# The last two stores of a kernel, written as four: one transfer for each batch

## The chip, the cores and the metric

The kernel runs on one core of a Trainium2 chip, as one program. The metric is the device time of that program in microseconds (us), taken as the median of several executions. One execution was also recorded by the hardware profiler; every duration below is from that record, and times inside it count from the start of its span.

## The reference

The inputs are float32. A linear attention without a softmax over 4 batches, 8 heads, 576 tokens and a head size of 64 is normalised per head, its heads are laid side by side to 2304 rows (4 batches of 576 tokens) of 512 columns, and two feed-forward layers follow:

```
kv  = einsum('bhsd,bhse->bhde', k, v)
o   = einsum('bhsd,bhde->bhse', q, kv)
o   = o / sqrt(mean(o*o, -1) + 1e-6) * g_norm
x   = o.transpose(0, 2, 1, 3).reshape(2304, 512)
g   = x @ w_gate;  h = g * sigmoid(g) * (x @ w_val);  x = h @ w_out        # inner width 1536
h   = x @ w_in;    y = softplus(h) @ w_out2                                # inner width 2048
```

The output is `y`, 2304 rows of 512 float32 numbers (2 KB a row); row `b*576 + s` is token `s` of batch `b`.

## The kernel before, in words

A batch has 576 tokens, which is 4 x 128 and 64 over. The kernel works on five token groups: groups 0 to 3 are the first 512 tokens of each batch (`T` = 512), and group 4 (`t == B`, with `B` = 4) is made of the four remainders, 64 tokens of each batch (`REM` = 64), 256 tokens side by side. In group 4, tokens 0 to 63 belong to batch 0, 64 to 127 to batch 1, and so on.

The stages are: attention, woven with the first feed-forward layer; the rest of that layer; and the second layer. The second layer runs over pairs of slices of its inner width (`jp`), for two batches at a time, and adds each slice's product into an accumulator in on-chip memory, `zacc`. For one step `m` of `ffn2_o`, TensorE makes a tile `pz` of 128 tokens by 512 columns in six matrix multiplications (L788 to L792, issued in the helper at L436), and VectorE adds it to `zacc` (L796). After the last pair (`jp == F2 // 2 - 1`) each step also puts a store into the queue of deferred work (L809, L810), which is released by the planner's clock just behind the addition.

The store has two forms. For a whole batch, L806 and L807 write the 128 rows of a step (for batches 2 and 3) or the 512 rows of four steps (for batches 0 and 1) in one transfer. For the remainders, `m` is 0 or 1 and the 128 partitions of `av[:, m, :]` hold 64 tokens of batch `2m` and 64 of batch `2m + 1`. L800 views the output as batches by tokens by columns, and L801 writes both remainders in one transfer. Group 4 comes last of all, so the two transfers of L801 are the last instructions of the kernel but the end of the program (L1002).

All stores and weight loads are issued on SP, in program order. SP waits before an issue where the program says so (for the data, and for a completion counter that an earlier transfer used: there are eight of these, `DMAHW0` to `DMAHW7`, used in turn).

Of the kernel before, what the change touches and what calls it, by code (L numbers as in the profile page):

```python
# [71 lines left out]
def tile_linear_attention_two_ffn(  # L72
# [19 lines left out]
    nc = tc.nc  # L92
    P = 128
    B, H, S, D = q.shape
    NP = H // 2
    NC = S // P
    REM = S - NC * P
# [4 lines left out]
    T = NC * P  # L102
# [26 lines left out]
    def defer(dt, f):  # L129
        heapq.heappush(queue, (now[0] + dt, next(serial), f))  # L130
# [8 lines left out]
    def need(made, key):  # L139
        while key not in made:  # L140
            heapq.heappop(queue)[2]()
        return made[key]
# [288 lines left out]
    def mm3(dst, steps, first=True, last=True, lo_rhs_last=True, check=True):  # L431
        n = 3 * len(steps)
        i = 0
        for (ah, al), (bh, bl) in steps:
            for a, b_ in ((ah, bh), (al, bh), (ah, bl)) if lo_rhs_last else ((ah, bh), (ah, bl), (al, bh)):
                nc.tensor.matmul(  # L436
                    dst, lhsT=a, rhs=b_, start=first and i == 0, stop=last and i == n - 1,
                    skip_group_check=not check)
                i += 1
        tick(n * 0.216 * dst.shape[-1] / 512)  # L440
# [17 lines left out]
    def acc_tile(gen, t):  # L458
        if (gen, t) not in acc:
            acc[gen, t] = accp.tile([P, KD, widths[t]], F32, tag=f"acc{t}", name=f"{gen}acc{t}")  # L460
        return acc[gen, t]
# [316 lines left out]
    def ffn2_o(jp, t):  # L778
        w = widths[t]
        gs = {}  # L780

        def step(m):
            if m == 0:
                for k_ in range(2):
                    gs[k_] = us2.pop((2 * jp + k_, t)), need(wt, ("p", 2 * jp + k_))
            a = acc_tile("z", t)
            av = a.rearrange("p k w -> p (k w)").rearrange("p (m e) -> p m e", e=DM)
            p = po.tile([P, DM], F32, tag="po", name=f"pz{jp}_{t}_{m}")  # L788
            mm3(p, [
                (tuple(g[:, m * P:(m + 1) * P] for g in gs[k_][0]), gs[k_][1])  # L790
                for k_ in range(2)
            ], lo_rhs_last=False)  # L792
            if jp == 0:
                nc.vector.tensor_copy(av[:, m, :], p)
            else:
                defer(ADD2, lambda: nc.vector.tensor_add(av[:, m, :], av[:, m, :], p))  # L796

            def store():
                if t == B:
                    rows = out.rearrange("(b s) e -> b s e", b=B)  # L800
                    nc.sync.dma_start(rows[2 * m:2 * m + 2, T:S, :], av[:, m, :])  # L801
                else:

                    n = NC if t < 2 else 1
                    if (m + 1) % n == 0:
                        rows = out[t * S:t * S + T, :].rearrange("(p c) e -> p c e", p=P)  # L806
                        nc.sync.dma_start(rows[:, m + 1 - n:m + 1, :], av[:, m + 1 - n:m + 1, :])  # L807

            if jp == F2 // 2 - 1:  # L809
                defer(ADD2, store)  # L810

        return [lambda m=m: step(m) for m in range(w // P)]
# [17 lines left out]
    with tc.manual_schedule():  # L830
# [65 lines left out]
        for t in range(NT - 1):  # L896
            if t + 1 < B:
                b = t + 2
# [108 lines left out]
```

## Time and profile before

| | |
|---|---|
| time, median of 3 runs | 920.41 us (920.1 to 923.91) |
| the profiled execution's own time | 920.24 us |
| its span, from the first to the last instruction | 918.5 us |
| TensorE busy | 885.1 us, 96% of the span |
| VectorE busy | 588.8 us, 64% |
| ScalarE, GpSimd busy | 353.1 us, 288.4 us |
| transfers | 114.00 MB, mean 124 GB/s |

A busy share is an average over the span. A change that touches only the end of the program is to be read from the end of the timeline, from what the transfer engines do there, and from what the program's last instruction waits for. The profiled execution's time is 1.74 us longer than its span; that part lies outside of the record.

### The profile page before, as it was taken

How to read it: one execution, taken by the hardware profiler on the slowest of the kernel's cores; microseconds unless marked ns; L12 is line 12 of the kernel's file. 1: busy time of each engine (PE TensorE's matmuls, PEld its weight loads, DVE VectorE, ACT ScalarE, POOL GpSimd, SP SyncE). 2: the span in 40 equal slices, each digit the busy share in tenths (PEclk: the TensorE clock that was granted, in tenths of full speed). 3: DMA queues.
4: the chain of work that ended last, by engine and by line, in shares of the span. 5: the costliest groups of instructions: out<-in, count | busy, mean ns of one | idle time of the engine just before them, and what ended most of it. 6: DMA issues, size and time to landing. Idle time of an engine off the chain costs nothing.

```text
span 918.5 us, 11708 instructions
## 1 busy us (share of the span) xinstructions
PE 885.1 (96%) x4352; PEld 740.8 (81%) x4352; DVE 588.8 (64%) x916; ACT 353.1 (38%) x615; POOL 288.4 (31%) x216
## 2 busy tenths in 40 slices
PE   6889999999999999999999999999999999999994
PEld 5668888888888888888888878888877888888883
DVE  2955357867868686787776745566687555545552
ACT  3634435333332323233232543444455444343430
POOL 0633211313131313122131633344444443333440
PEclk9999999999999999999999999999999999999998
DMA  9975202143251605051534134444445433343102
GB/s 274 253 137 117 92 1 70 59 149 128 80 193 37 226 28 183 34 196 46 161 115 161 68 119 140 170 146 160 161 139 175 168 138 120 111 137 122 40 12 103
DMA packets 83932, 114.00 MB, mean 124 GB/s; under 512 B 27556, under 2 KB 56228, under 8 KB 83620
## 3 DMA queue, kind: packets, MB, share of 16 engines
q1 hardware_dynamic: 83716, 113.27, 38.6%
q8 instruction: 34, 0.56, 0.3%
q14 instruction: 22, 0.18, 0.1%
q10 hardware_dynamic: 160, 0.00, 0.0%
HBM read 91.75 MB, written 21.50 MB: 123 GB/s over the span
## 4 chain that ended last, share of the span: by engine, by line
PE 83%; DVE 6%; issue 3%; SPq 2%; POOL 2%; ACT 1%; DMA 1%; POOLq 0%; DVEq 0%; ACTq 0%
PE pz L436 20%; PE pv L436 15%; PE pg L436 15%; PE py L436 15%; PE hY L436 8%; PE hZ L436 4%; PE hr L436 2%; PE hX L436 2%; PE pa L366 1%; POOL b L620 1%; DMA qr<-in_q_dram 1%; PE kvp L318 1%; SPq L181 1%; DVE yacc L496 1%; POOL gl L698 1%
## 5 line engine op out<-in xcount | busy, mean ns | idle before, releaser
L496 DVE TENSOR_TENSOR yacc<-yacc,py 128x512 f32<-128x512 f32 (+1 forms) x220 | 136.4, 629 | 53.6 <-PE py L436 53.0
L796 DVE TENSOR_TENSOR zacc<-zacc,pz 128x512 f32<-128x512 f32 x126 | 85.9, 683 | 109.4 <-PE pz L436 109.2
L698 POOL TENSOR_TENSOR gl<-c,gh 128x512 fp32r<-128x512 f32 x64 | 88.5, 1383 | 189.7 <-ACT gh L697 145.4
L436 PE MATMUL pz<-pl,gh 128*128 128x512 f32 x288 | 112.5, 391 | 2.0 <-POOL pl L285 2.0
L436 PE MATMUL pz<-ph,gl 128*128 128x512 f32 x288 | 112.4, 390 | 0.6 <-POOL gl L698 0.6
L436 PE MATMUL pz<-ph,gh 128*128 128x512 f32 x288 | 112.4, 390 | 0.0
L478 ACT CAST uh<-u 128x512 fp32r<-128x512 f32 (+1 forms) x60 | 34.7, 578 | 173.8 <-DVE u L475 173.8
L436 PE MATMUL hY<-b,wh 128*128 128x512 f32 x384 | 97.6, 390 | 0.9 <-DVE c L726 0.9
L436 PE MATMUL py<-uh,oh 128*128 128x512 f32 (+1 forms) x240 | 89.7, 374 | 1.3 <-DVE yacc L496 1.3
L436 PE MATMUL pv<-xh,vh 128*128 128x512 f32 (+1 forms) x240 | 90.1, 375 | 0.0
L436 PE MATMUL pg<-xh,gh 128*128 128x512 f32 (+1 forms) x240 | 90.0, 375 | 0.0
L436 PE MATMUL pg<-xl,gh 128*128 128x512 f32 (+1 forms) x240 | 88.5, 369 | 0.5 <-DVE xl L404 0.5
L436 PE MATMUL py<-uh,ol 128*128 128x512 f32 (+1 forms) x240 | 88.6, 369 | 0.0
L436 PE MATMUL pv<-xh,vl 128*128 128x512 f32 (+1 forms) x240 | 88.6, 369 | 0.0
L436 PE MATMUL pg<-xh,gl 128*128 128x512 f32 (+1 forms) x240 | 88.5, 369 | 0.0
L436 PE MATMUL pv<-xl,vh 128*128 128x512 f32 (+1 forms) x240 | 88.4, 368 | 0.0
L436 PE MATMUL py<-ul,oh 128*128 128x512 f32 (+1 forms) x240 | 88.3, 368 | 0.0
L436 PEld LDWEIGHTS hY<-b,wh 128*128 128x128 f32 x384 | 71.6, 188 | 15.9 <-DVE c L726 1.3
L436 PEld LDWEIGHTS pz<-pl,gh 128*128 128x128 f32 x288 | 54.2, 188 | 13.2 <-POOL pl L285 2.9
L436 PEld LDWEIGHTS pz<-ph,gl 128*128 128x128 f32 x288 | 54.1, 188 | 13.0 <-POOL gl L698 1.8
L479 DVE TENSOR_TENSOR ul<-u,uh 128x512 fp32r<-128x512 f32 (+1 forms) x60 | 38.8, 647 | 39.1 <-ACT uh L478 39.1
L436 PEld LDWEIGHTS pz<-ph,gh 128*128 128x128 f32 x288 | 54.1, 188 | 10.9 <-ACT ph L282 0.3
(115 smaller groups left out, 1643.1 us busy)
## 6 DMA issues: line engine op xcount, KB each, us to landing
pr<-in_moe_w_out_dram SPq DMA_DIRECT2D x32, 512.0 KB, 4.3
wh<-w2d SPq DMA_DIRECT2D x32, 512.0 KB, 4.3
wh<-w2d SPq DMA_DIRECT2D x64, 256.0 KB, 2.9
ir<-in_moe_w_in_dram SPq DMA_DIRECT2D x16, 512.0 KB, 5.7
w2d<-kh SPq DMA_DIRECT2D x32, 256.0 KB, 2.0
w2d<-kl SPq DMA_DIRECT2D x32, 256.0 KB, 2.4
gr<-in_moe_w_gate_dram SPq DMA_DIRECT2D x12, 512.0 KB, 7.2
vr<-in_moe_w_val_dram SPq DMA_DIRECT2D x12, 512.0 KB, 7.2
```

The source lines that it names most:

```text
L181: nc.sync.dma_start(kr.rearrange("p h c d -> p h (c d)"), ks.rearrange("h (p c) d -> p h (c d)", p=P))
L318: nc.tensor.matmul(pk[:, hp, :], lhsT=kt[:, c, i:i + 2, :].rearrange("p h d -> p (h d)"), rhs=vt[:, i:i + 2, c * D:(c + 1) * D], start=(c ...
L366: nc.tensor.matmul(pv[p0:p0 + n, hp, :], lhsT=qt[:, hp, p0:p0 + n], rhs=kvm[bb][:, hp, :], start=True, stop=True,)
L436: nc.tensor.matmul(dst, lhsT=a, rhs=b_, start=first and i == 0, stop=last and i == n - 1, skip_group_check=not check)
L478: nc.scalar.copy(uh, u)
L479: (nc.gpsimd if UL1 == "g" else nc.vector).tensor_sub(ul, u, f32(uh))
L496: defer(ADD1, lambda: nc.vector.tensor_add(a[:, d, :], a[:, d, :], p))
L620: (nc.gpsimd if BLO[n][int(i[1])] == "g" else nc.vector).tensor_sub(t[:, 1], src(), f32(t[:, 0]))
L698: nc.gpsimd.tensor_sub(lo, l, f32(hi))
L796: defer(ADD2, lambda: nc.vector.tensor_add(av[:, m, :], av[:, m, :], p))
```

## The change

In the branch for the remainders, the one transfer of 128 rows is replaced by two transfers of 64 rows, one for each of the two batches in the tile. Each takes 64 partitions of `av[:, m, :]` and writes 64 neighbouring rows of the output, 128 KB. The branch runs twice (`m` = 0 and 1), so two transfers of 256 KB become four of 128 KB. The bytes and where they go are the same.

```
             def store():
                 if t == B:
-                    rows = out.rearrange("(b s) e -> b s e", b=B)
-                    nc.sync.dma_start(rows[2 * m:2 * m + 2, T:S, :], av[:, m, :])
+                    for i in range(2):
+                        r0 = (2 * m + i) * S + T
+                        nc.sync.dma_start(out[r0:r0 + REM, :], av[REM * i:REM * (i + 1), m, :])
                 else:
```

The end of SP's program before; `zacc_6515` and `zacc_6605` are the accumulators of batches 3 and 2, `zacc_5214` that of the remainders, the last figures are the shape of the transfer, and the brackets name the counters that SP waits for:

```order
L807 DMA out_dram<-zacc_6515 128x512 [waits DMAHW2_49,DVE_49]
L807 DMA out_dram<-zacc_6515 128x512 [waits DMAHW3_49,DVE_49]
L807 DMA out_dram<-zacc_6515 128x512 [waits DMAHW4_49,DVE_49]
L807 DMA out_dram<-zacc_6515 128x512 [waits DMAHW5_49,DVE_49]
L807 DMA out_dram<-zacc_6605 128x512 [waits DVE_49] x2
L807 DMA out_dram<-zacc_6605 128x512 [waits DMAHW0_49,DVE_49]
L807 DMA out_dram<-zacc_6605 128x512 [waits DMAHW1_49,DVE_49]
L801 DMA out_dram<-zacc_5214 2x64x512 [waits DMAHW2_49,DVE_49]
L801 DMA out_dram<-zacc_5214 2x64x512 [waits DMAHW3_49,DVE_49]
L1002 UNCONDITIONAL_BRANCH
```

And the same end of SP's program with the change (the lines of the source are one further on):

```order
L808 DMA out_dram<-zacc_6605 128x512 [waits DMAHW0_49,DVE_49]
L808 DMA out_dram<-zacc_6605 128x512 [waits DMAHW1_49,DVE_49]
L802 DMA out_dram<-zacc_5214 64x512 [waits DMAHW2_49,DVE_49]
L802 DMA out_dram<-zacc_5214 64x512 [waits DMAHW3_49]
L802 DMA out_dram<-zacc_5214 64x512 [waits DMAHW4_49,DVE_49]
L802 DMA out_dram<-zacc_5214 64x512 [waits DMAHW5_49]
L1003 UNCONDITIONAL_BRANCH
```

The last two entries became four. The first of each pair waits for VectorE's addition, the second only for a completion counter whose last user is eight transfers back. Nothing else moved on any engine.

## Rows read from the trace of the kernel before

**Rows 1.** The page's busy time by engine; the core's span and granted TensorE clock.

```profile
PE 885.1 (96%) x4352; PEld 740.8 (81%) x4352; DVE 588.8 (64%) x916; ACT 353.1 (38%) x615; POOL 288.4 (31%) x216
...
core 0: 918.5 us, clock 0.995
```

**Rows 2.** Timeline of the end: start us, us, engine, line, operation, tiles, [idle before].

```profile
904.46 0.39 PE L436 MATMUL pz<-ph,gl 128*128 128x512 f32 x1
904.88 0.69 DVE L796 TENSOR_TENSOR zacc<-zacc,pz 128x512 f32<-128x512 f32 x1 [0.67 <-PE pz L436]
...
902.88 0.33 SPq L807 DMA_DIRECT2D out_dram<-zacc  x1
...
904.24 0.66 SPq L801 DMA_DIRECT2D out_dram<-zacc  x1
...
905.60 0.53 SPq L801 DMA_DIRECT2D out_dram<-zacc  x1
```

**Rows 3.** What SP waited for at the end: us in total, times, longest.

```profile
SPq L1002 <- DMA out_dram<-zacc: 11.2, 1, 11.2
```

**Rows 4.** Stretches of the end: length, busy by engine, PEclk, DMA share, GB/s.

```profile
903.50:904.45 0.95, 0.95 (x5) 0.77 (x5) 0.69 (x1) 0.00 (x0) 0.00 (x0) 1.00 0.73 276
904.45:905.25 0.80, 0.40 (x2) 0.00 (x0) 0.36 (x1) 0.00 (x0) 0.00 (x0) 1.00 0.00 0
905.25:907.50 2.25, 0.00 (x0) 0.00 (x0) 0.32 (x1) 0.00 (x0) 0.00 (x0) 1.00 0.12 25
...
908.00:916.75 8.75, 0.00 (x0) 0.00 (x0) 0.00 (x0) 0.00 (x0) 0.00 (x0) 0.58 0.13 51
916.75:917.00 0.25, 0.00 (x0) 0.00 (x0) 0.00 (x0) 0.00 (x0) 0.00 (x0) 0.50 0.11 41
917.00:918.50 1.50, 0.00 (x0) 0.00 (x0) 0.00 (x0) 0.00 (x0) 0.00 (x0) 0.50 0.00 0
```

**Rows 5.** Packets of transfers: stretch 903.45 to 904.6 (L807's last), then 904.6 to 919.

```profile
DMA packets 144, 0.26 MB, mean 228 GB/s; under 512 B 16, under 2 KB 16, under 8 KB 144
...
DMA packets 260, 0.52 MB, mean 36 GB/s; under 512 B 4, under 2 KB 4, under 8 KB 260
```

**Rows 6.** ScalarE's own transfer queue, and its only transfers (64x1 each), whole span.

```profile
q10 hardware_dynamic: 160, 0.00, 0.0%
...
gcol<-in_g_norm_dram ACTq DMA_DIRECT2D x2, 0.2 KB, 4.1
```

**Rows 7.** Issues of the stores by line: ns min/median/max; us from issue to landing.

```profile
L807 SPq DMA_DIRECT2D out_dram<-zacc x10: 332/332/344, 702.7 to 902.9; - x10
L801 SPq DMA_DIRECT2D out_dram<-zacc x2: 526/590/655, 904.2 to 905.6; - x2
...
DMA to landing us min/median/max: 2.0/2.1/5.0
...
DMA to landing us min/median/max: 2.2/2.2/2.2
```

**Rows 8.** The first load of the kernel, its landing, and the copy that waits for it.

```profile
0.73 0.45 SPq L181 DMA_DIRECT2D kr<-in_k_dram  x1
...
kr<-in_k_dram SPq DMA_DIRECT2D x1, 512.0 KB, 4.0
...
4.73 0.40 ACT L185 COPY k<-kr 128x256 f32<-128x256 f32 x1 [2.72 <-DMA kr<-in_k_dram]
```

**Rows 9.** Two loads into 64 partitions each, issued one behind the other, and their landing.

```profile
63.40 0.61 SPq L204 DMA_DIRECT2D kvr<-in_k_dram  x1
64.05 0.63 SPq L204 DMA_DIRECT2D kvr<-in_v_dram  x1
...
DMA to landing us min/median/max: 4.9/5.0/5.2
```

**Rows 10.** Earlier L807 stores whose counters the third and fourth new transfers wait for.

```profile
896.08 0.33 SPq L807 DMA_DIRECT2D out_dram<-zacc  x1
...
897.44 0.33 SPq L807 DMA_DIRECT2D out_dram<-zacc  x1
```

## The prediction

> **What bounds the kernel now.** I read the cores first: one core, 918.5 us, mean granted clock 0.995, so no throttled stage colours the figures [rows 1]. The page gives TensorE 96% of the span [rows 1], and that would end the reading for any edit that touches only stores. But the chain of waits ends with VectorE's last addition, and the timeline shows that one from 904.88 to 905.57 [rows 2], 12.9 us before the span does. So I read the end by itself. SP issues the last two stores (L801) at 904.24 and 905.60; the second issue is over at 906.13 [rows 2]. Then SP waits 11.2 us for a transfer from `zacc` [rows 3], to 906.13 + 11.2 = 917.33, and 918.50 - 917.33 = 1.17 us of program end follow. No compute engine works in that time. The last 11.2 us belong to the two stores alone.
>
> What these do is in the stretches: from 908.00 to 916.75 the transfer engines are busy for 0.13 of their time and move 51 GB/s [rows 4]. There are 16 engines, and 0.13 x 16 = 2.1: two engines work, 25.5 GB/s each, and fourteen stand idle. Two stores of 262,144 bytes at 51 GB/s need 10.3 us, which is the tail. The packets say the same. A store of L807 leaves 144 packets: 128 rows of 2 KB and 16 small ones. The two stores of L801 leave 260: 256 rows and 4 small ones, so 2 each [rows 5]. Taking a small packet as one engine's report of its end, L807 ran on 16 engines and L801 on 2. L807's shape is 128x512 and L801's 2x64x512, so 2 is the outer dimension.
>
> **Part 1: how many engines a 64-row transfer gets.** No store here has 64 rows outermost. The nearest shape is the load of `gcol`, two transfers of 64x1, alone in ScalarE's queue: 160 packets [rows 6], less 2 x 64 for the rows leaves 32, so 16 each. I take 16 engines for the new stores, 4 rows each.
>
> **Part 2: the issues.** Two are removed (0.66 and 0.53 us) and four put in. The 128x512 store takes 0.33 us to issue [rows 7], the two-batch one 0.53 to 0.66, a load into 64 partitions, cut into pieces by head, 0.61 and 0.63 with 64.05 - 64.01 = 0.04 us between two [rows 9]. I take 0.33, since the new shape is plain rows like L807's; bounds are 0.33 and 0.63. The first pair then holds SP from 904.24 to 904.94 (905.54 at most), before the second addition releases the second pair at 905.60 either way. So the first pair's issues are hidden behind VectorE, and 905.60 stays. The second pair is issued at 905.60 and 905.60 + 0.33 + 0.04 = 905.97 (906.27 at most). The added waits are for counters of the stores issued at 896.08 and 897.44 [rows 10], landed some 2 us later, over 5 us before they are asked for: nothing. Behind them on SP stands only the program's end.
>
> **Part 3: the landing.** The time to landing counts from the start of the issue: the first load starts at 0.73, is given 4.0 us, and the copy that waits for it starts at 4.73 [rows 8]. A store of 256 KB by L807 lands 2.0 to 2.2 us after that start (the 5.0 are of the 1 MB stores) [rows 7]. I take 2.1 us for the last 128 KB, though it has half the bytes, because the 128 KB just ahead of it are in the same engines: landing at 905.97 + 2.1 = 908.07. Lower bound: data of the last L807 store flow from 903.50 to 904.45 [rows 4], which is 0.62 us after the issue at 902.88, for 0.95 us, and it has landed at 902.88 + 2.2 = 905.08, 0.63 us after the data. By that pace the pair's data flow from 905.60 + 0.62 = 906.22 to 907.17 and have landed at 907.80. Upper bound from a row, however far: the 64-partition loads took 5.2 us at most, in a busier stretch and in pieces of a head [rows 9]; 906.27 + 5.2 = 911.47. I stay by L807, which writes the same tensor from the same engines in rows of the same length.
>
> The first pair, issued 1.36 us earlier, has its data out by 904.24 + 0.62 + 0.95 = 905.81, before the second pair's begin.
>
> **The sum.** The landing moves from 917.33 to 908.07: 9.26 us less. The span is 908.07 + 1.17 = 909.24, and with the 920.24 - 918.50 = 1.74 us outside it 910.98 us. The median of the runs is 0.17 above the profiled execution: 911.15, which I round to 911.2 us. Bounds of the terms: 907.80 gives 910.9 on the same scale, slow issues (906.27 + 2.2 = 908.47) 911.6, the far row 914.6. What is late next is the landing of any last store at all, some 2 us, then VectorE's addition, then TensorE; none can be reached by this edit.
>
> **A rule against it.** The rows show the 128-row store at 276 GB/s over its 0.95 us [rows 4], and no store from 64 partitions. The Trainium skill, "SBUF — State Buffer", sections "Door 1: The DMA port swizzle" and "Can I just issue two DMAs to hit both halves?", says that 64 neighbouring partitions reach only half of the 16 ports through which transfers enter and leave, and that two transfers, one for each half, serialize, so that only one transfer over all 128 partitions has the full rate. By that rule each new transfer goes at half rate; without it, at the pace of L807. The two-batch store of before did span 128 partitions, and the trace has it at 51 GB/s, so here the rule cannot be the whole story.
>
> **The rivals.**
>
> *Half rate.* The four transfers run on many engines, but each moves 128 KB in the 0.95 us in which L807's moved 256 KB, one after another. The first pair's data flow from 904.86 for 1.90 us to 906.76, the second pair's to 908.66; with 0.63 us to land 909.29, the span 910.46, the time 912.4 on the median's scale. This is also what the rule of the page above would give. For it: nothing in the trace shows 64 partitions at full rate. Against it: L801 had each of its two engines at 25.5 GB/s on 64 partitions of its own, no slower than a sixteenth of L807's flow (276 / 16 = 17). It is still 8 us better than before.
>
> *The split doesn't spread.* The transfers stay on two engines, because the count follows something else than the outer dimension (the bytes or the partitions). The same 524,288 bytes go at 51 GB/s from about the same start, and the time is 920.4, no change. Against it: the 16 small packets a transfer of `gcol` [rows 6]. For it: that is a load, of 4 bytes a row.
>
> *One engine, slower.* The 64 rows of each store are one unbroken piece of 128 KB in the output, where L807's rows and L801's two batches have gaps. If that piece is taken as one row, a transfer gets one engine, and if it is always the same, 524,288 bytes go at 25.5 GB/s: 20.6 us from 905.25 [rows 4], with 917.33 - 917.00 = 0.33 to land, 926.2; the time is 929.3, slower by 9. It decides as soon as the engines that take part fall below two. Against it: the shape in SP's program is still 64x512, and `gcol`'s 64 numbers were an unbroken piece too and left 16 small packets a transfer.
>
> **How the numbers follow.** My forecast 0.64, half rate 0.27, somewhere between half rate and two engines (4 engines, say) 0.03, no spread 0.04, one engine 0.02. The forecast's own bounds are 910.9 to 911.6, half rate gives 912.4; with 0.7 us for the runs' own scatter below and above, the range is 910.2 to 913.1, which leaves out the last three cases and the far row. What a measurement can tell from no change is about 0.5%, 4.6 us, and both first cases clear that by far: faster 0.94, same 0.04, slower 0.02.
>
> **What the changed kernel's profile would show.** Four issues of about 0.33 us, at 904.24, 904.61, 905.60 and 905.97; after 905.6 a short stretch with a DMA share near that of L807's stores instead of 0.13 over 11 us; 320 packets there (256 rows and 64 small) instead of 260; SP's last wait about 1.8 us instead of 11.2; the span near 909.2; everything before 904.2 as it was. Half rate would show as twice the length of data at half the GB/s. A count of small packets under 64 would say that fewer engines took part, and then the step that fails is part 1; a count of 64 with a late landing puts it at part 3.

## The result and the profile after

The changed kernel takes 911.62 us in the median of four runs (911.47 to 914.42), beside 920.96 us for the kernel before in four runs: 9.34 us less, a ratio of 0.9889 with a 95% interval of 0.9872 to 0.9907. The forecast was 911.2 us, with a range of 910.2 to 913.1. The profiled execution took 911.74 us, with a span of 909.9.

The end of SP's and VectorE's work in the changed kernel, as the timeline has it (start, duration, engine, line, operation; the line of SP's stores is now L802); these rows answer to [rows 2], and the last one is the span:

```profile
905.38 0.69 DVE L796 TENSOR_TENSOR zacc<-zacc,pz 128x512 f32<-128x512 f32 x1 [0.67 <-PE pz L436]
...
904.74 0.55 SPq L802 DMA_DIRECT2D out_dram<-zacc  x1
...
904.74 1.19 SPq L802 DMA_DIRECT2D out_dram<-zacc  x2
...
906.09 1.12 SPq L802 DMA_DIRECT2D out_dram<-zacc  x2
...
906.62 0.59 SPq L802 DMA_DIRECT2D out_dram<-zacc  x1
...
core 0: 909.9 us, clock 1.000
```

The last addition ends at 905.38 + 0.69 = 906.07, and 909.90 - 906.07 = 3.83 us of span follow, where the kernel before had 12.93. This distance, from the last addition to the span's end, is called the tail below. What lies ahead of it varies from one execution to the next (the spans of the kernel before run from 918.6 to 921.2 us beside one of the groups below), so the tail shows the stores better than the total does.

What SP waited for at the end (total, times, longest), where [rows 3] had one wait of 11.2 us:

```profile
SPq L1003 <- DMA out_dram<-zacc: 1.7, 3, 0.6
```

And the packets of the stretch from 905.22 to 909.57, where the second row of [rows 5] had 260 with 4 small ones:

```profile
DMA packets 320, 0.52 MB, mean 121 GB/s; under 512 B 64, under 2 KB 64, under 8 KB 320
```

There are 64 small packets (under 512 B) for four stores, 16 each. With one such packet from each engine that took part, as the prediction reads them, 16 engines work where two did. The stretches (length, busy time by engine, granted clock, share of the transfer engines, GB/s) answer to [rows 4]:

```profile
904.25:904.90 0.65, 0.65 (x4) 0.55 (x3) 0.46 (x1) 0.00 (x0) 0.00 (x0) 1.00 0.98 372
904.90:905.82 0.92, 0.44 (x2) 0.02 (x1) 0.44 (x1) 0.00 (x0) 0.00 (x0) 1.00 0.02 7
905.82:907.20 1.38, 0.00 (x0) 0.00 (x0) 0.25 (x1) 0.00 (x0) 0.00 (x0) 1.00 0.85 186
907.20:908.55 1.35, 0.00 (x0) 0.00 (x0) 0.00 (x0) 0.00 (x0) 0.00 (x0) 1.00 0.89 199
908.55:909.90 1.35, 0.00 (x0) 0.00 (x0) 0.00 (x0) 0.00 (x0) 0.00 (x0) 1.00 0.00 0
```

The first row is the last 128-row store: 372 GB/s with the engines 0.98 busy. The third and fourth are the four 64-row stores: 186 and 199 GB/s with the engines 0.85 and 0.89 busy. The engines are nearly as full, but they carry half as much. And the issues (ns) and landings (us) of the new stores; a landing counts from the start of the issue to the report that the data have arrived:

```profile
L802 SPq DMA_DIRECT2D out_dram<-zacc x4: 472/570/594, 904.7 to 906.6; - x4
...
DMA to landing us min/median/max: 2.3/2.3/2.4
```

An issue takes 0.47 to 0.59 us and not L807's 0.33, and the landing comes 2.3 to 2.4 us after its start, where L807's 256 KB stores had 2.0 to 2.2. (The 2.2 in the last line of [rows 7] is that of the last L807 store. No row gives a landing for L801; by [rows 3] SP waited for it until 917.33, over 11 us after the last issue began.) Ahead of the tail the program is the same. Its last addition came 0.50 us later in this execution than in the one before.

### The profile page after: what moved, and what is told of

It reads as the page before. It is cut to its first block, busy times and chain, and to the rows that moved or that the text cites. A ratio compares the mean times of both kernels' runs of the same rounds, so it can differ in the third digit from the quotient of the medians.

```text
span 909.9 us, 11710 instructions
## 1 busy us (share of the span) xinstructions
PE 885.3 (97%) x4352; PEld 741.3 (81%) x4352; DVE 589.3 (65%) x916; ACT 353.0 (39%) x615; POOL 288.2 (32%) x216
## 4 chain that ended last, share of the span: by engine, by line
PE 85%; DVE 6%; issue 3%; POOL 2%; ACT 1%; DMA 1%; SPq 0%; POOLq 0%; DVEq 0%; ACTq 0%
PE pz L436 20%; PE pv L436 15%; PE pg L436 15%; PE py L436 15%; PE hY L436 8%; PE hZ L436 4%; PE hr L436 2%; PE hX L436 2%; PE pa L366 1%; PE kvp L318 1%; DMA kvr<-in_v_dram 1%; POOL b L620 1%; PE pq L349 1%; DVE yacc L496 1%; PE kvp L327 1%
```

## The experiments

Two things were to be settled: whether the number of engines, taken to follow the outer dimension, is the whole gain, and why the new stores have half the rate and slower issues.

**The changed kernel again**, as the base of the first group.

> The changed kernel again, as the base of this group. Its first profile had the last addition end 3.8 us before the span (12.9 in the kernel before), the last four stores' data at some 205 GB/s with the transfer engines all busy, and issues of 0.47 to 0.59 us. Both theories expect the same again, within 0.2 us of each of these, and 911 to 912 us.

Ratio 0.9904 (0.9885 to 0.9922), span 910.3, last addition at 906.43: a tail of 3.87 us, issues 0.47 to 0.59 us, landings 2.3 to 2.4 us. The picture repeats.

**64 partitions spread over all 128.** The transpose ahead of the first layer writes the two batches' tokens alternately, which permutes the tokens of group 4 from there on. So the two stores take the even and the odd partitions, and each still writes 64 neighbouring rows.

```
-            nc.tensor.transpose(px[:, hp, :], x[:, hp, :], ident)
+            po_ = px[:, hp, :] if c < NC else px[:, hp, :].rearrange("p (s j) -> p j s", j=2)
+            nc.tensor.transpose(po_, x[:, hp, :], ident)
...
-                        nc.sync.dma_start(out[r0:r0 + REM, :], av[REM * i:REM * (i + 1), m, :])
+                        nc.sync.dma_start(out[r0:r0 + REM, :], av[i::2, m, :])
```

> The remainder tokens of two batches are laid alternately (even partitions one batch, odd partitions the other), so each of the four stores is still 64 rows and still one unbroken 128 KB of the output, but its 64 partitions are spread over all 128. Theory A (the rate halves because a transfer's partitions all lie in one half of the 128): data of the pair at 340 to 400 GB/s, in about 0.7 us instead of 1.25, last addition to span's end 3.2 to 3.5 us. Theory B (64 rows a transfer, or the unbroken piece of output, halve the rate): 200 to 220 GB/s as in the changed kernel and 3.8 us.

Ratio 0.9901 (0.9884 to 0.9917). The last addition ends at 905.91 + 0.69 = 906.60, the span at 910.2: a tail of 3.60 us.

```profile
905.91 0.69 DVE L797 TENSOR_TENSOR zacc<-zacc,pz 128x512 f32<-128x512 f32 x1 [0.67 <-PE pz L437]
...
core 0: 910.2 us, clock 0.997
```

Three stretches of the last pair's data (length, busy time by engine, granted clock, share of the transfer engines, GB/s):

```profile
907.85:908.10 0.25, 0.00 (x0) 0.00 (x0) 0.00 (x0) 0.00 (x0) 0.00 (x0) 1.00 1.02 385
908.10:908.35 0.25, 0.00 (x0) 0.00 (x0) 0.00 (x0) 0.00 (x0) 0.00 (x0) 1.00 0.11 33
908.35:908.60 0.25, 0.00 (x0) 0.00 (x0) 0.00 (x0) 0.00 (x0) 0.00 (x0) 0.74 0.80 303
```

The four stores' issues (ns) and landings (us):

```profile
L803 SPq DMA_DIRECT2D out_dram<-zacc x4: 478/572/588, 905.3 to 907.2; - x4
...
DMA to landing us min/median/max: 2.0/2.1/2.1
```

The rate is back at 385 GB/s, the landing at 2.0 to 2.1 us, with the same 64 rows and the same unbroken 128 KB of output. Theory B falls, and theory A holds for the rate: it halves when all the partitions lie in one half of the 128. The step of two is not what gives the full rate, since L807's 128 neighbouring partitions have it too (393 GB/s in a quarter of a microsecond); 64 neighbouring partitions across the middle would be the last check, and were not tried. The issues stay slow (0.48 to 0.59), so they are another matter; and the stretch at 33 GB/s shows that the transfer engines now pause between one store's data and the next's. The tail of 3.60 us lies outside A's 3.2 to 3.5: it shrank by 0.2 to 0.3 us only. Where the data pause between two stores, the rate is not what sets the end; as far as these rows show, the slow issues do.

**One store of 64 x 2 x 512**, in the same alternate layout.

```
-                    for i in range(2):
-                        r0 = (2 * m + i) * S + T
-                        nc.sync.dma_start(out[r0:r0 + REM, :], av[REM * i:REM * (i + 1), m, :])
+                    rows = out.rearrange("(b s) e -> s b e", b=B)
+                    nc.sync.dma_start(rows[T:S, 2 * m:2 * m + 2, :], av[:, m, :])
```

> The same alternate layout, but one store of 256 KB for both batches with the 64 tokens outermost (64 x 2 x 512) instead of two. Theory A: 16 engines (16 small packets a store), full rate, 340 to 400 GB/s, one issue of 0.35 to 0.65 us, landing 2.0 to 2.2 us after it starts, so last addition to span's end about 3.2 us, 0.6 us less than the changed kernel. Theory B, if it is the number of rows that counts: the same 3.2 us; if it is pieces of the output that are unbroken: about 3.8. If the number of engines did not follow the outer dimension, a long tail as in the kernel before, up to 12.9 us.

Ratio 0.9906 (0.9889 to 0.9923), last addition at 907.65 + 0.69 = 908.34, span 911.9: a tail of 3.56 us.

```profile
907.65 0.69 DVE L797 TENSOR_TENSOR zacc<-zacc,pz 128x512 f32<-128x512 f32 x1 [0.67 <-PE pz L437]
...
core 0: 911.9 us, clock 0.995
```

The packets of both stores:

```profile
DMA packets 288, 0.52 MB, mean 121 GB/s; under 512 B 32, under 2 KB 32, under 8 KB 288
```

One stretch of the first store's data, in the columns of before:

```profile
908.59:908.84 0.25, 0.00 (x0) 0.00 (x0) 0.00 (x0) 0.00 (x0) 0.00 (x0) 1.00 1.04 393
```

Issues (ns) and landings (us):

```profile
L802 SPq DMA_DIRECT2D out_dram<-zacc x2: 562/590/618, 907.0 to 908.4; - x2
...
DMA to landing us min/median/max: 2.4/2.4/2.4
```

Two transfers of the same 256 KB as in the kernel before, but with 64 tokens outermost and not two batches: 16 small packets each, 393 GB/s, and the long tail is gone. So it is the outer dimension and not the split that saves the time. The tail is longer than the 3.2 us of theory A. The issue of 0.56 to 0.62 us is inside the 0.35 to 0.65 expected; what was mis-sized is the landing, 2.4 us after the issue's start and not 2.0 to 2.2.

**The second store of a pair from ScalarE.**

```
-                    for i in range(2):
+                    for i, eng in enumerate((nc.sync, nc.scalar)):
...
-                        nc.sync.dma_start(out[r0:r0 + REM, :], av[REM * i:REM * (i + 1), m, :])
+                        eng.dma_start(out[r0:r0 + REM, :], av[REM * i:REM * (i + 1), m, :])
```

> The changed kernel with the second store of each pair issued by ScalarE, which is idle then, so that the two issues of a pair run side by side. Theory C (the second issue, some 0.6 us behind the first, sets the end): last addition to span's end 3.8 - 0.5 = 3.3 us. Theory A beside it: with both halves in flight at once the data flow at 340 to 400 GB/s together and the end is 3.2 us. Theory D (the rate sets the end, the pair is serialized at 205 GB/s whoever issues it): data for 1.25 us from about 0.7 us after the addition, 0.4 us to land, and the program's end, 3.4 to 3.8 us.

Ratio 0.9902 (0.9888 to 0.9917), last addition at 906.66, span 910.4: a tail of 3.74 us, inside theory D's range; C and A are out. Its last pair, in the stretch of its data and in two quarters of a microsecond of it:

```profile
908.16:908.41 0.25, 0.00 (x0) 0.00 (x0) 0.00 (x0) 0.00 (x0) 0.00 (x0) 1.00 1.11 213
908.66:908.91 0.25, 0.00 (x0) 0.00 (x0) 0.00 (x0) 0.00 (x0) 0.00 (x0) 1.00 0.78 295
...
907.80:908.95 1.15, 0.00 (x0) 0.00 (x0) 0.00 (x0) 0.00 (x0) 0.00 (x0) 1.00 0.86 228
```

The two issues start together, 0.6 us are saved there, and the tail gains only 0.1 us: the pair as a whole goes at 228 GB/s, little over the 186 and 199 of before, and the landings take up to 2.7 us. The rate is not one figure: it begins at some 213 GB/s and ends at 295. Why was not tried.

**Both: alternate partitions, and the second store from ScalarE.** Its edit is the two above together.

> Alternate layout (64 partitions spread over all 128) and the second store of each pair issued by ScalarE. In the alternate layout alone the last addition ended 3.60 us before the span with gaps between the four stretches of data, so the issues and not the rate set the end there; with ScalarE alone 3.74 us, with the data at the lower rate while the halves were not yet both in flight. If the second issue (about 0.6 us later) is what is left, both together give 3.60 - 0.6 = 3.0 to 3.2 us. Rival: two queues issuing at once slow each other's landing (2.3 to 2.7 us were seen instead of 2.0 to 2.1), and the end is 3.4 to 3.7 us.

Ratio 0.9913 (0.9891 to 0.9935), last addition at 908.83, span 912.2: a tail of 3.37 us, the shortest of all. It is outside the 3.0 to 3.2 expected, and next to the 3.4 to 3.7 of the rival, by which two queues slow each other's landing. The data of the first pair, as a stretch:

```profile
908.70:909.40 0.70, 0.00 (x0) 0.00 (x0) 0.13 (x1) 0.00 (x0) 0.00 (x0) 1.00 0.96 363
```

The landings (us) of the last pair:

```profile
DMA to landing us min/median/max: 2.0/2.2/2.3
```

The first pair's 256 KB take 0.70 us at 363 GB/s, and its data no longer pause. The landings go up to 2.3 us (2.6 in the first pair), where 2.0 to 2.1 were seen with one queue, so the rival has a part in it. The gain over the changed kernel is 0.5 us of tail, less than a ratio of whole times can show: its interval and that of the changed kernel overlap, and no version is shown to beat the changed kernel.

**Only the second pair split.** The store of `m` = 0 stays as it was (2 x 64 x 512), that of `m` = 1 is two of 64 rows.

```
-                if t == B:
+                if t == B and m == 0:
+                    rows = out.rearrange("(b s) e -> b s e", b=B)
+                    nc.sync.dma_start(rows[2 * m:2 * m + 2, T:S, :], av[:, m, :])
+                elif t == B:
```

> One part alone: the first of the two stores stays as one transfer of two batches, only the second is two transfers of 64 rows. If the number of engines is what cost the time, the first store keeps two engines for 262,144 bytes at 51 GB/s, 5.1 us from about 0.3 us before the last addition ends, and the second pair's rows on those two engines queue behind it: last addition to span's end 6.4 to 7.0 us (12.9 before, 3.8 with both split), and 2 + 32 = 34 small packets. If only the last store counted, it would be 3.8 us.

One run: 919.21 us, last addition at 909.17, span 917.4: a tail of 8.23 us, with the 2 + 32 = 34 small packets expected. That is between 12.9 and 3.8, as the number of engines wants it, but longer than the 6.4 to 7.0 expected. The stretches of the tail:

```profile
909.00:910.50 1.50, 0.00 (x0) 0.00 (x0) 0.17 (x1) 0.00 (x0) 0.00 (x0) 1.00 0.19 34
910.50:912.00 1.50, 0.00 (x0) 0.00 (x0) 0.00 (x0) 0.00 (x0) 0.00 (x0) 0.76 0.43 60
912.00:913.00 1.00, 0.00 (x0) 0.00 (x0) 0.00 (x0) 0.00 (x0) 0.00 (x0) 0.50 0.79 197
```

The landing (us) of the two split stores, issued at 909.20 and about 0.6 us later:

```profile
DMA to landing us min/median/max: 6.6/6.7/6.9
```

Two things were not foreseen. The two-engine store starts slowly, at 34 GB/s and not 51. And the stores of 64 rows behind it, which could run on fourteen idle engines, move most of their data only from about 912 on, 2 to 3 us after their issue, where the first 64-row store of the changed kernel had data flowing 1.1 us after its own (904.74 to 905.82). So a store on two engines holds up the ones behind it. The engines' share of 0.43 from 910.50 to 912.00 is more than two of sixteen, so more than two were busy by then, at 60 GB/s in all. Why was not tried.

**62 and 2 rows.** Each 64 rows in two pieces, so that the outer dimension is 62.

```
-                        nc.sync.dma_start(out[r0:r0 + REM, :], av[REM * i:REM * (i + 1), m, :])
+                        for p0, p1 in ((0, REM - 2), (REM - 2, REM)):
+                            nc.sync.dma_start(out[r0 + p0:r0 + p1, :], av[REM * i + p0:REM * i + p1, m, :])
```

> Each 64 rows are written as 62 and 2 rows, so nearly the same four transfers, with an outer dimension of 62. If a transfer takes the largest number of engines up to 16 that divides its outer dimension, 62 gets 2 engines and 2 gets 2: 8 x 2 = 16 small packets, about 51 GB/s, last addition to span's end 12 to 13.5 us as in the kernel before. If the rows are spread over as many engines as there are, evenly or not, it is some 4 to 6 us (the four more issues of 0.5 us, two of them behind the addition), and more than 60 small packets.

One run: 922.88 us, last addition at 907.57 + 0.69 = 908.26, span 921.1: a tail of 12.84 us, the kernel before over again.

```profile
907.57 0.69 DVE L796 TENSOR_TENSOR zacc<-zacc,pz 128x512 f32<-128x512 f32 x1 [0.67 <-PE pz L436]
...
core 0: 921.1 us, clock 0.993
```

Its packets:

```profile
DMA packets 272, 0.52 MB, mean 39 GB/s; under 512 B 16, under 2 KB 16, under 8 KB 272
```

Two stretches of its data:

```profile
907.50:912.00 4.50, 0.03 (x1) 0.00 (x0) 0.69 (x1) 0.00 (x0) 0.00 (x0) 1.00 0.12 33
912.00:919.00 7.00, 0.00 (x0) 0.00 (x0) 0.00 (x0) 0.00 (x0) 0.00 (x0) 0.50 0.13 51
```

16 small packets for eight transfers, 2 each. 62 rows get two engines and 64 get sixteen. The Trainium skill, "DMA: Bandwidth & Descriptors", section "Why a DMA increments its semaphore by 16 and not by 1", has the rule that a transfer takes the largest number of engines up to 16 that divides the outermost dimension (the outermost that is not 1) of both its sides. The counts of small packets here agree with it: 2 a store for 2x64x512 and for the 62 and 2 rows, 16 for 64 and for 128 rows.

**The earlier 128-row stores cut**, off the path that sets the end.

```
-                        nc.sync.dma_start(rows[:, m + 1 - n:m + 1, :], av[:, m + 1 - n:m + 1, :])
+                        cut = {(3, 0): 64, (3, 1): 96, (3, 2): 112, (2, 1): 32, (2, 2): 64}.get((t, m), P)
+                        for p0, p1 in ((0, cut), (cut, P)):
...
```

> The changed kernel with six of the eight 128-row stores ahead of the last ones cut into two transfers, by rows (64 and 64, 96 and 32, 112 and 16, 32 and 96, 64 and 64) and once by columns (128 x 256 twice); nothing of it is on the path that sets the end, and the pieces of rows have gaps between them in the output. Theory E (an issue costs 0.33 us when the transfer has 128 rows and more, about 0.5 to 0.6, when it has fewer): 0.33 for each 128 x 256, 0.45 to 0.6 for 64, 96, 112, 32 and 16 rows alike. Theory F (the unbroken 128 KB of output costs it): 0.33 for all of these. Theory G (it is the second issue close behind the first that costs): 0.33 for the first and 0.5 to 0.6 for the second piece, the halves by columns too. Data of 64 rows from one half at 200 to 220 GB/s here too if the half of the partitions sets the rate; at 380 if the unbroken output did. Last addition to span's end 3.8 us by all.

One run, 912.12 us, tail 3.97 us (last addition at 906.33, span 910.3). The timeline of the issues: 64 and 64 rows, 96, 112, 128 x 256 twice, 32 and 96, and the other 64 and 64 (the second pieces of 32 and 16 rows, behind the 96 and the 112, took 0.42 and 0.43):

```profile
894.12 0.55 SPq L814 DMA_DIRECT2D out_dram<-zacc  x1
894.71 0.60 SPq L814 DMA_DIRECT2D out_dram<-zacc  x1
895.48 0.45 SPq L814 DMA_DIRECT2D out_dram<-zacc  x1
...
896.84 0.32 SPq L814 DMA_DIRECT2D out_dram<-zacc  x1
...
898.20 0.35 SPq L812 DMA_DIRECT2D out_dram<-zacc  x1
898.59 0.43 SPq L812 DMA_DIRECT2D out_dram<-zacc  x1
...
900.92 0.33 SPq L814 DMA_DIRECT2D out_dram<-zacc  x1
901.30 0.41 SPq L814 DMA_DIRECT2D out_dram<-zacc  x1
...
902.27 0.48 SPq L814 DMA_DIRECT2D out_dram<-zacc  x1
902.80 0.59 SPq L814 DMA_DIRECT2D out_dram<-zacc  x1
```

The stretch with the data of the first 64 and 64 rows:

```profile
895.25:896.25 1.00, 1.00 (x6) 0.84 (x5) 0.33 (x2) 0.00 (x0) 0.00 (x0) 1.00 0.87 193
```

Theory F falls: with gaps in the output 64 rows still take 0.48 to 0.60, and their data flow at 193 GB/s, so the unbroken piece has no part in either. E and G hold in part only. In pieces of one size the second costs 0.05 to 0.11 us more than the first (0.43 after 0.35 for the halves by columns), but 96 rows cost less as a second piece (0.41) than as a first (0.45). And 64 rows cost more than 112 (0.32), 96, and 32 (0.33 as a first piece). The 62 rows of the run before, in nearly the same place but on two engines, took 0.29 to 0.39. What makes 64 rows the dearest stays open.

## Why the prediction was right, point by point

The time was right by its main step. Two smaller terms were too short, a third was too long by about as much as either, and the rate was wrong in a way that the price chosen for it covered up: that the time came within 0.5 us is in part luck.

*The tail belongs to two engines* was right, and so was *part 1*: 16 small packets a store, as `gcol`'s count had it [rows 6]. The experiments close the other doors. The split is not needed (one store of 64 x 2 x 512 has 3.56 us of tail), and it is not enough (62 and 2 rows have 12.84 us). The rivals of no spread and of one engine are out.

*Part 2*, the issues: 0.33 us was wrong, 0.47 to 0.59 is what they take. The upper bound of 0.63, from the 64-partition loads [rows 9], held, and those were the nearer row: 64 rows, where L807's transfers have 128. That the first pair hides behind VectorE held with 0.16 us to spare (904.74 + 1.19 = 905.93; the next starts at 906.09). The last issue starts 0.55 us after the last addition, 0.15 later than forecast. It does not set the end, though: the data run on from 905.82 to 908.55 with the engines 0.85 and 0.89 busy, so those of the last store wait for the ones ahead of them. The run with the second store from ScalarE moved that issue forward by 0.6 us and gained 0.1.

*Part 3*, the landing: 2.1 us was taken from L807, 2.3 was measured, and the step that failed is that the new stores move at L807's pace. They don't; the rival of half rate had the mechanism right, and the prediction's own sign of it, data for twice as long at half the GB/s, is what the stretches show. The argument against it, 25.5 GB/s for each of L801's two engines, does not carry over to sixteen at once, which have 199 / 16 = 12 GB/s each here. The rule of half the ports, from the page "SBUF — State Buffer" of the Trainium skill, section "Door 1: The DMA port swizzle", agrees with this trace (186 and 199 GB/s, not 372). Its other section, "Can I just issue two DMAs to hit both halves?", by which only one transfer over all 128 partitions has the full rate, is too narrow here: 64 partitions spread over both halves move at up to 385. Its warning against splitting in two did not cost the gain, since the alternative here had two engines.

Half rate was forecast at 912.4 us, though, with a tail of 910.46 - 905.57 = 4.89 us, and 3.83 came. Its price was mis-sized: both cases took 0.95 us for L807's 256 KB, at 276 GB/s, from a stretch that began some 0.2 us before the data did. Two stretches of that store in the kernel before, finer than [rows 4]:

```profile
903.50:904.00 0.50, 0.50 (x3) 0.39 (x3) 0.47 (x1) 0.00 (x0) 0.00 (x0) 1.00 0.57 217
904.00:904.25 0.25, 0.25 (x3) 0.20 (x2) 0.21 (x1) 0.00 (x0) 0.00 (x0) 1.00 1.04 393
```

The middle of such a store goes at 372 to 393 GB/s, some 0.7 us in all. Half of that is 186 to 197 GB/s, some 0.7 us for each new store, and that is what was measured: between the 0.95 / 2 = 0.48 us of the forecast and the 0.95 us of the rival. So the forecast had the wrong mechanism at a price too high for it, the rival the right one at a price too high, and the time came out between, nearer to the forecast.

The sum: the last issue 0.15 us later and its landing 0.2 longer than forecast, the program's end 909.90 - (906.62 + 2.3) = 0.98 us and not 1.17. These are +0.15, +0.2 and -0.19, so the tail is 3.83 us where 909.24 - 905.57 = 3.67 was forecast. The rest of the span's difference, 909.9 to 909.24, is the last addition, which came 0.5 us later in this execution.

## What to carry to other kernels

Look at the end of a kernel by itself: 96% of TensorE hid 11 us in which two of sixteen transfer engines worked, and a DMA share of 0.13 with SP in a single long wait is how that looks. Count the small packets of a transfer to see how many engines it got, and choose the outermost dimension by that; in this kernel 64 and 128 gave sixteen engines, 62 and 2 gave two. When a pace is read from a stretch, take out the part in which nothing flows yet, or two cases that differ by a factor of two can't be told apart.

## What the runs showed of the hardware that was not expected

- A store from partitions 0 to 63 or 64 to 127 moved at 186 to 199 GB/s with all 16 engines; one from every second partition at up to 385. Two queues that send one half each did not lift it much (228 over the pair, 295 at its end).
- Issuing a store of 64 rows took SP 0.47 to 0.60 us, whichever partitions and whatever piece of the output it had; 128 rows took 0.33 to 0.43, and 62 rows, on two engines, 0.29 to 0.39.
- Two stores on sixteen engines behind one on two landed 6.6 to 6.9 us after their issue, and 2.3 to 2.4 without it in front.
- Stores on two engines start slowly: 25 GB/s in their first 2.25 us in the kernel before, 51 later [rows 4]. With 62 and 2 rows it was 33 GB/s until 912.00 and 51 from there on; SP's last issue ended at 911.91. The cause was not looked for.
